# An mLSTM cell and a multiplicative feed-forward block: own outputs copied by ScalarE, y by DRAM from the eleventh unit, denominators in four passes

## The chip, the cores and the metric

The kernel runs on one core of a Trainium2 chip. The metric is the device time of one launch in microseconds (us); lower is better. All times below are us unless marked ns. The engines are named as the profile names them: PE is TensorE, DVE VectorE, ACT ScalarE, POOL GpSimd, SP SyncE, which issues most of the DMAs.

## What is computed

The reference has two parts. The first is a recurrence over 768 time steps for 4 batches of 8 heads of 40 columns:

```python
    for t in range(S):
        m_new = np.maximum(f_gate[:, :, t] + m, i_gate[:, :, t])
        f_stab = np.exp(f_gate[:, :, t] + m - m_new)
        i_stab = np.exp(i_gate[:, :, t] - m_new)
        C = f_stab * C + i_stab * outer(v[t], k[t])
        n = f_stab * n + i_stab * k[t]
        denom = max(abs(n . q[t]), 1.0)
        y[t] = sigmoid(o_gate[t]) * (C q[t]) / denom
```

The second takes x, which is y as 3072 tokens of 320 columns, and computes `((x @ w1) * (x @ w2)) @ w3 @ w_out`, with 1024 columns between. All is float32.

## The kernel before

**Units and stages.** The recurrence is cut into 24 units, one for each batch b and each 128 time steps c; unit n has c, b = divmod(n, 4). The main loop, `for s in range(len(n_up))`, has 32 turns; a turn is called a stage here. Stage s does the following for unit s: scores (q against k), weighting, state update. In the same stage it does for unit s - 1 the outputs, and for unit s - 2 or s - 3 the handing over of y to the feed-forward part. Beside this, a stage runs a share of the feed-forward part, by tables written out by hand: `n_up` (blocks of x @ w1 and x @ w2), `n_down` (blocks of the last product), `n_seven` and `n_out` (blocks done with seven products in place of eight), `n_cvt` (conversions of the weights w3 and w_out) and `n_fetch` (their loads). The order of the trace is the order on each engine's queue (`in_order` for PE, `keep_order` for the other engines), so an instruction that waits holds up all that stands behind it on its engine. This holds for SP's queue of DMAs too.

**Outputs of a unit** (`outputs`, `quarter_work`). PE leaves two things in the PSUM tile `cell[1]`: `pi`, what the state gives, and `ph`, what the unit's own 64-step halves give. DVE multiplies `pi` by the gate `gT` into `h` (L423), adds `ph` in four quarters of 64x164 (L430), and then makes the denominator. The last of 41 columns of each head is n . q, because the last column of `vbuf` is 1. L438 clears the sign bit, L440 takes max with 1 and doubles, L441 takes the reciprocal, L443 multiplies it by (o + 1), where o is a tanh, and L445 multiplies by `h` and writes `y`. Between these steps stand DVE's reading of the scores (L397), and the two state sums (L404, L414), the second of which waits for a product by POOL (L335).

**Handing over y.** There are two ways. For units under `NY` (15), `x_trans` turns y on PE, three 128x128 transposes into PSUM tile `px` (L95), and ACT copies it to `xT` (L486); POOL first doubles the last 64 columns (`twice`, L476). In stages 10 and later, stage s does this for unit s - 3, as the first PE work of the stage. For units from `NY` on, `send` writes y to DRAM (four DMAs on SP, L456 and L458), `get_back` reads it back in blocks (four DMAs, L465), and DVE turns 32x32 blocks (`x_turn`, L472). Stage s does this for unit s - 2: `send` is SP's first work of the stage, `get_back` stands behind the loads of k, v and o for unit s + 2, and `x_turn` stands on DVE behind `quarter_work`.

**Who reads xT.** One `xT` tile holds four units (a group). The 24 blocks of `ups` each read two units, a half of a group: blocks 16 to 19 read units 8 and 9, blocks 20 to 23 read units 10 and 11. By `n_up` stages 2 to 5 do one block and stages 6 to 15 two, so blocks 20 and 21 are done in stage 14. Groups 3 to 5 (units 12 to 23) are done by seven products: `token_sums` (L666, DVE) makes sums of a group's `xT` in stages 17, 21 and 25.

**SP's order in a stage** is written in the loop: `send(s - 2)`, `load_u(s + 3)` (tile pw, L159), k and v and o of unit s + 2 (L139, L153), `get_back(s - 2)`, `load_turned(s + 2)` (eight DMAs, tiles gates or q_all, L148), and last the fetches of w3 (tile raw, L184), eight DMAs a stage up to stage 12. A fetch needs a free `raw` buffer. One is freed by each conversion (`convert`: DVE L199, L200, then L248), and the conversions of a stage stand on DVE behind `turn` (L317, two transposes that make kT and qT of unit s + 1).

## Time and profile before

| | before |
|---|---|
| runs | 425.51, 426.51 and 427.06; median 426.51 |
| profiled execution | span 425.84; no time of its own beside the span is given |
| PE busy | 414.1 of 425.8 (97%), 5353 matmuls |
| DVE, ACT, POOL busy | 313.5 (74%), 150.1 (35%), 154.3 (36%) |
| mean granted TensorE clock | 0.996 |
| DMA | 51.15 MB, 120 GB/s in the mean |

The profile is of one execution. The span is from its first to its last instruction. A row of a timeline gives the start, the length, the engine, the line, what is written and read, and in brackets how long the engine was idle before it and what ended that; SPq is the DMA queue of SP, whose rows are the issuing and not the transfer. Rows of several instructions are merged (x4, x8), and their length reaches from the first's start to the last's end. A granted clock of 1.00 is TensorE's full speed.

Stages are found by their PE work. Stage 12 begins with the px transposes at 142.95, stage 13 at 158.94, stage 14 at 174.22, stage 15 at 189.51, stage 16 at 204.80, stage 17 at 220.07.

### The profile page before, as it was taken

The numbers are of one execution on the slowest core, as the hardware profiler recorded it, in microseconds if no ns is written. First come the engines' busy times: TensorE is split into PE (matmuls) and PEld (weight loads), VectorE is DVE, ScalarE is ACT, GpSimd is POOL, SyncE is SP. The second block draws the span as 40 slices with busy tenths as digits, with TensorE's granted clock in tenths as the row PEclk, the third lists the DMA queues.
The fourth block names the chain that finished last, engine by engine and source line by source line (L and its number), as shares of the span: only waits on it lengthen the run. The fifth ranks groups of instructions, "written<-read, shape, count | busy, mean of one in ns | idle before, by whom it ended". The sixth has DMA issues, their size and how long they took to land.

```text
span 425.8 us, 13079 instructions
## 1 busy us (share of the span) xinstructions
PE 414.1 (97%) x5353; PEld 335.3 (79%) x5353; DVE 313.5 (74%) x635; ACT 150.1 (35%) x404; POOL 154.3 (36%) x211
## 2 busy tenths in 40 slices
PE   7989989999999999999999999999999999999996
PEld 4768878888688788787777778788778879888896
DVE  6676986888949779778736966596868699575971
ACT  4766865567723623630433313032311110210000
POOL 4421342233303303303307751546453587542100
PEclk9989999999999999999999999999999999999999
DMA  8999998598977776985425675756421120000001
GB/s 186 204 173 245 214 144 140 134 193 180 215 183 154 166 182 135 181 164 105 89 80 130 153 141 121 142 133 117 87 44 36 35 39 2 31 2 31 2 32 62
DMA packets 135211, 51.15 MB, mean 120 GB/s; under 512 B 109360, under 2 KB 126960, under 8 KB 135152
## 3 DMA queue, kind: packets, MB, share of 16 engines
q1 hardware_dynamic: 131552, 46.29, 53.9%
q10 hardware_dynamic: 3600, 4.03, 2.7%
q8 instruction: 42, 0.69, 0.7%
q14 instruction: 17, 0.14, 0.1%
HBM read 44.50 MB, written 5.80 MB: 118 GB/s over the span
## 4 chain that ended last, share of the span: by engine, by line
PE 53%; issue 20%; DVE 7%; POOL 7%; SPq 7%; DMA 5%; ACT 1%; POOLq 0%; DVEq 0%
PE cell L92 17%; PE pa L92 12%; PE o L92 8%; PE pb L92 8%; PE p L92 3%; POOL pw L308 3%; SPq L184 3%; DVE w3T L666 2%; PE pt L95 1%; POOL vw L330 1%; SPq L148 1%; DMA raw<-in_moe_w_dram 1%; PE fill L92 1%; POOL raw L659 1%; POOL state L335 1%
## 5 line engine op out<-in xcount | busy, mean ns | idle before, releaser
L335 POOL TENSOR_TENSOR state<-state,decay 128x164 f32<-128x164 f32 x40 | 20.0, 500 | 154.8 <-DVE state L404 129.0
L92 PE MATMUL pa<-xT,w 128*128 128x256 f32 x240 | 60.4, 382 | 0.0
L92 PEld LDWEIGHTS pa<-xT,w 128*128 128x128 f32 x240 | 44.4, 190 | 6.8 <-DVE h L430 0.4
L303 ACT ACTIVATE pw<-pw,aT 128x64 f32<-128x64 f32 x184 | 46.4, 339 | 3.2 <-ACT o_sb L741 1.9
L92 PE MATMUL pb<-xT,w 128*128 128x256 f32 x192 | 45.4, 379 | 0.0
L729 POOL TENSOR_TENSOR ab<-ab,a_sb 128x512 f32<-128x512 f32 x22 | 29.4, 1356 | 32.2 <-DVE ab L684 32.2
L92 PEld LDWEIGHTS pb<-xT,w 128*128 128x128 f32 x192 | 36.4, 190 | 5.0
L711 POOL TENSOR_TENSOR wo<-wo 128x512 f32<-128x512 f32 x22 | 27.4, 1268 | 29.8 <-DVE wo L686 29.8
L92 PE MATMUL pa<-xT,wr 64*64 64x256 f32 x384 | 37.0, 386 | 0.5 <-DVE wr L200 0.5
L92 PE MATMUL wp<-wo,w3T 128*128 128x320 f32 x128 | 35.9, 433 | 1.1 <-DVE ab L639 0.6
L308 POOL TENSOR_SCALAR_AFFINE_SELECT pw<-pw 64x512 f32<-64x512 f32 x48 | 35.8, 746 | 3.0 <-ACT pw L303 1.2
L92 PE MATMUL pb<-xT,wr 64*64 64x256 f32 x384 | 36.4, 380 | 0.0
L92 PE MATMUL cell<-w3o,ab 128*128 128x320 f32 x128 | 35.4, 432 | 0.0
L638 ACT ACTIVATE a_sb<-pa 128x512 f32<-128x512 f32 x24 | 14.3, 598 | 59.0 <-PE pb L92 59.0
L639 DVE TENSOR_TENSOR ab<-pb,a_sb 128x512 f32<-128x512 f32 x24 | 16.4, 688 | 23.2 <-ACT a_sb L638 22.8
L92 PEld LDWEIGHTS wp<-wo,w3T 128*128 128x128 f32 x128 | 23.8, 190 | 10.5 <-DVE ab L639 0.8
L92 PEld LDWEIGHTS cell<-w3o,ab 128*128 128x128 f32 x128 | 24.3, 190 | 9.5
L92 PEld LDWEIGHTS pa<-xT,wr 64*64 64x64 f32 x384 | 18.9, 132 | 15.4 <-issue 8.8
L686 DVE SCALAR_TENSOR_TENSOR a_sb<-pa,wo 128x512 f32<-128x512 f32 x12 | 8.3, 689 | 29.8 <-PE pa L92 29.8
L430 DVE TENSOR_TENSOR h<-cell,h 64x164 f32<-64x164 f32 x88 | 28.6, 326 | 1.6
L92 PE MATMUL po<-w3o,ab 128*128 128x320 f32 x96 | 26.4, 433 | 0.0
L92 PEld LDWEIGHTS po<-w3o,ab 128*128 128x128 f32 x96 | 18.1, 190 | 7.3
(180 smaller groups left out, 846.4 us busy)
## 6 DMA issues: line engine op xcount, KB each, us to landing
raw<-in_moe_w_dram SPq DMA_DIRECT2D x64, 128.0 KB, 3.4
kbuf<-in_k_dram SPq DMA_DIRECT2D x24, 160.0 KB, 4.5
v_all<-in_v_dram SPq DMA_DIRECT2D x24, 160.0 KB, 4.9
o_in<-in_o_gate_dram SPq DMA_DIRECT2D x24, 160.0 KB, 4.8
pw<-U_d SPq DMA_DIRECT2D x28, 128.0 KB, 3.5
raw<-in_moe_w_dram SPq DMA_DIRECT2D x5, 512.0 KB, 6.7
raw<-in_moe_w_out_dram SPq DMA_DIRECT2D x8, 320.0 KB, 4.1
gates<-in_k_dram SPq DMA_DIRECT2D x28, 80.0 KB, 2.5
```

Of the source, the lines that this page charges most:

```text
L92: in_order(nc.tensor.matmul(out, lhsT=lhsT, rhs=rhs, start=start, stop=stop))
L184: nc.sync.dma_start(out=dst, in_=src)
L303: nc.scalar.activation(out=pw[:, h, :], in_=src[:, h, :], func=AF.Exp, bias=aT[:, c, b * H + h:b * H + h + 1])
L308: nc.gpsimd.affine_select(out=pw[r], in_=pw[r], compare_op=OP.is_ge, fill=0.0, base=0, pattern=[[0, H], [1, L]], channel_multiplier=-1)
L335: nc.gpsimd.tensor_tensor(out=new, in0=old, op=OP.mult, in1=decay[:, b * NP:(b + 1) * NP, 2 * c + x:2 * c + x + 1] .to_broadcast([P, NP, D1]))
L430: nc.vector.tensor_tensor(out=part, in0=ph[x][halves[e]], in1=part, op=OP.add)
L638: nc.scalar.mul(out=a_sb, in_=pa, mul=UP ** -2)
L639: nc.vector.tensor_tensor(out=ab_t[gr][j][:, fs[0]:fs[-1] + 1, t0:t0 + a_sb.shape[-1]], in0=pb, in1=a_sb, op=OP.mult)
L666: nc.vector.tensor_tensor(out=dst, in0=p, in1=q, op=OP.subtract)
L686: nc.vector.scalar_tensor_tensor(out=out, in0=p, scalar=UP ** -2, in1=q, op0=OP.mult, op1=OP.add)
L711: aside_by.tensor_tensor(out=kept[j][:, 1:4:2], in0=kept[j][:, 1:3], in1=kept[j][:, 3:4].to_broadcast([128, 2, TH]), op=OP.add)
L729: aside_by.tensor_tensor(out=t[:, f:FO:FH, :], in0=t[:, f:FO:FH, :], in1=a, op=OP.mult)
```

## The change

Three things change, and the diff is short enough to be shown whole.

1. `N_OWN = 10`: for units from 10 on, the gated `pi` goes to the tile `y` (as a scratch place), four ACT copies bring the quarters of `ph` from PSUM to `h`, and one DVE addition of 128x328 puts the two together. `y` is allocated at the start of `outputs` for all units.
2. `NY` goes from 15 to 10: units 10 to 14 too hand over y by DRAM.
3. For all units, the denominator is made in other steps. The last column of `vbuf` is 2 in place of 1, so the last column of `h` is 2 n . q. The steps are: reciprocal; the larger of the result and its negative; a pass over 128x320 that takes the minimum with 0.5 and multiplies into `h`; a pass over 128x320 that multiplies by (o + 1) into `y`.

```diff
-    N_DIAG = 2
+    N_DIAG, N_OWN = 2, 10
...
-    NY = 15
+    NY = 10
...
         h = sb.tile([P, H, D1], FP, name="h", tag="h")
-        nc.vector.tensor_tensor(out=h.rearrange("p (n two) d -> p two n d", two=2), in0=pi,
+        y = y_t[n] = sb.tile([P, DM + REM], FP, name="y", tag="y")
+        before = y[:, 0:H * D1].rearrange("p (h d) -> p h d", d=D1) if n >= N_OWN else h
+        nc.vector.tensor_tensor(out=before.rearrange("p (n two) d -> p two n d", two=2), in0=pi,
                                 in1=gT[:, c, hs].rearrange("p (n two) -> p two n", two=2).unsqueeze(3)
                                 .to_broadcast([P, 2, NP, D1]), op=OP.mult)
         if n < N_DIAG:
             nc.vector.tensor_tensor(out=h, in0=ph, in1=h, op=OP.add)
-        for x, e in quarters if n >= N_DIAG else ():
+        if n >= N_OWN:
+            for x, e in quarters:
+                nc.scalar.copy(out=h[halves[x], 0:H // 2] if x == e else h[halves[x], H // 2:H], in_=ph[x][halves[e]])
+            nc.vector.tensor_tensor(out=h, in0=before, in1=h, op=OP.add)
+        for x, e in quarters if N_DIAG <= n < N_OWN else ():
             part = h[halves[x], 0:H // 2] if x == e else h[halves[x], H // 2:H]
             nc.vector.tensor_tensor(out=part, in0=ph[x][halves[e]], in1=part, op=OP.add)
...
-            yield V.tensor_scalar(out=den.bitcast(U32), in0=h[:, :, D:D1].bitcast(U32), scalar1=0x7FFFFFFF, scalar2=None,
-                            op0=OP.bitwise_and)
-            yield V.tensor_scalar(out=den, in0=den, scalar1=1.0, scalar2=2.0, op0=OP.max, op1=OP.mult)
-            yield V.reciprocal(out=den, in_=den)
-            e = o_t.pop(n)
-            nc.vector.scalar_tensor_tensor(out=e, in0=e, scalar=1.0, in1=den.to_broadcast([P, H, D]), op0=OP.add, op1=OP.mult)
-            y_t[n] = sb.tile([P, DM + REM], FP, name="y", tag="y")
-            yield nc.vector.tensor_tensor(out=y_t[n][:, 0:DM].rearrange("p (h d) -> p h d", d=D), in0=h[:, :, 0:D],
-                                           in1=e, op=OP.mult)
+            yield V.reciprocal(out=den, in_=h[:, :, D:D1])
+            yield V.scalar_tensor_tensor(out=den, in0=den, scalar=-1.0, in1=den, op0=OP.mult, op1=OP.max)
+            v = h[:, :, 0:D]
+            yield V.scalar_tensor_tensor(out=v, in0=den.to_broadcast([P, H, D]), scalar=0.5, in1=v, op0=OP.min, op1=OP.mult)
+            yield V.scalar_tensor_tensor(out=y[:, 0:DM].rearrange("p (h d) -> p h d", d=D), in0=o_t.pop(n), scalar=1.0,
+                                         in1=v, op0=OP.add, op1=OP.mult)
...
-        nc.gpsimd.memset(vbuf[i][:, :, D:D1], 1.0)
+        nc.gpsimd.memset(vbuf[i][:, :, D:D1], 2.0)
```

The order of the changed kernel's instructions shows what this does to each engine. PE loses 15 transposes (five groups of px). ACT loses five copies of px and gains 14 groups of four copies of 64x164, each group ahead of the exponentials (L303) of the next unit. POOL loses five copies. SP gains 20 DMAs to DRAM and 20 back, in stages 12 to 16, at the places named above. DVE gains five block transposes.

## The prediction

> **What bounds the kernel now.** I read the page first, for shares and slices:

> ```profile
> PE 414.1 (97%) x5353; PEld 335.3 (79%) x5353; DVE 313.5 (74%) x635; ACT 150.1 (35%) x404; POOL 154.3 (36%) x211
> ...
> PE   7989989999999999999999999999999999999996
> ```

> PE is busy in nearly every slice. The view of waits, asked for PE alone, says how little it waits for others; these are the two entries that the change touches:

> ```profile
> PE px L95 <- DVE y L445: 1.2, 1, 1.2
> ...
> PE pa L92 <- DVE w3T L666: 0.4, 1, 0.4
> ```

> So from stage 2 on the span is PE's queue, and time is won by taking work from that queue or lost by making it wait. A faster DVE is worth nothing by itself. The question for each edit is therefore: what does PE wait for then, and when does that come? PE's timeline at the start of stage 14:

> ```profile
> 174.22 0.55 PE L95 MATMUL px<-ident,y 128*128 128x128 f32 x3
> 174.61 4.47 PE L92 MATMUL wp<-wo,w3T 128*128 128x320 f32 x16
> 178.92 1.46 PE L92 MATMUL pa<-xT,w 128*128 128x256 f32 x6
> ```

> The px here turns unit 11. The pa that starts at 178.92 is block 20 of `ups`, the first reader of unit 11's xT. This is the place that decides, as follows.

> **Part 1, work taken from PE (gain).** A px group holds the queue from 174.22 to 174.61, 0.39. Units 10 to 14 lose theirs: 5 x 0.39 = 1.95. Of these, units 10 and 11 stand ahead of block 20, units 12 to 14 behind it.

> **Part 2, own outputs by ACT, and four passes (DVE and ACT).** DVE's timeline for unit 10 before:

> ```profile
> 142.60 0.49 DVE L423 TENSOR_TENSOR h<-cell,gT 128x328 f32<-128x328 f32 x1
> 143.12 1.34 DVE L430 TENSOR_TENSOR h<-cell,h 64x164 f32<-64x164 f32 x4
> ...
> 146.15 0.33 DVE L414 TENSOR_TENSOR state<-cell,state 128x164 f32<-128x164 f32 x1 [0.47 <-POOL state L335]
> 146.40 0.76 DVE L443 SCALAR_TENSOR_TENSOR o_in<-o_in,den 128x320 f32<-128x320 f32 x1
> 147.20 0.82 DVE L445 TENSOR_TENSOR y<-h,o_in 128x320 f32<-128x320 f32 x1
> ```

> The four additions (1.34) go. In the changed kernel's order with its waits, ACT's first copy waits for DVE's multiply of the same unit (the old L423), though it reads only `ph`; so the copies do not lie beside the multiply but after it. No row has this copy. Bounds: the exponentials of 128x64 follow each other every 0.25 (2.01 for eight), the po copies of 128x320 take 0.43; four copies cost 1.0 to 1.7. I take 4 x 0.29 = 1.2, interpolated by columns between the exponentials' 0.25 and the kT and qT copies of 128x512, which start 0.48 apart. The addition of 128x328 is like L423, 0.5. So h is ready 1.7 after the multiply in place of 1.34: 0.35 later. The short passes lose one (0.17). The long pass now stands ahead of L414 and covers its 0.47 wait for POOL. Net per unit from 10 on: +0.35 - 0.17 - 0.47 = -0.3; below 10: -0.6. PE waits for neither, except at 242, where `token_sums` made it wait 0.4 (0.58 with the start-up of the matmul). DVE comes 0.3 earlier there, and xT of unit 15 is no longer behind; I take -0.5.

> ACT's exponentials of stage 11 began at 141.85 and would begin at 143.1 + 1.2 = 144.3, 2.4 later. Behind them stands the copy of px for unit 9, which ended at 146.82 and would end at 149.2, while PE wants it at 148.34: 0.8 of waiting, in stage 12. It lies ahead of block 20 and is swallowed by the larger wait there. The first-stage wait of 1.2 for y shrinks by some 0.6, but conversions held by loads (ACT waits for raw at 42.48 and 44.48) stand before stage 3's end; I take 0.1.

> [...] Here L443 (two float32 sources) at 24.60 took 0.49 and L445, a tensor_tensor, took 0.49 at 25.13. [...]

> **Part 3, y by DRAM for units 10 and 11 (loss).** SP's timeline, stages 11 to 13, then stage 17, which already works in the new way:

> ```profile
> 151.06 3.89 SPq L184 DMA_DIRECT2D raw<-in_moe_w_dram  x8
> 155.06 1.09 SPq L159 DMA_DIRECT2D pw<-U_d  x2
> ...
> 167.00 3.89 SPq L184 DMA_DIRECT2D raw<-in_moe_w_dram  x8
> 171.01 1.09 SPq L159 DMA_DIRECT2D pw<-U_d  x2
> ...
> 224.90 1.28 SPq L456 DMA_DIRECT2D y_d<-y  x2
> 226.22 1.15 SPq L458 DMA_DIRECT2D y_d<-y  x2
> ...
> 231.05 3.05 SPq L465 DMA_DIRECT2D yb<-y_d  x4
> ```

> ```profile
> 235.87 0.58 DVE L472 STREAM_TRANSPOSE xT<-yb 128x384 f32<-128x384 f32 x1
> ```

> Unit 15's way from the first `send` to the block transpose took 224.90 to 235.87, 10.97; unit 16's 238.72 to 249.54, 10.8. Between stand four sends (2.5), the loads of pw, k, v and o, and the reads back, which land behind o. The new units have the same DMAs between, so 10.9 is the price of the way. SP does not reach it early, because the stage before ends with the raw fetches, which wait for DVE's conversions (first group of four DMAs after the first L200, second after the second).

> Step by step. Stage 11's fetches end 0.3 earlier, at 154.65. Unit 10: send at 154.65, block transpose at 154.65 + 10.9 = 165.55, done 166.1. DVE is free for it at 163.99 - 0.3 + 0.7 (the late px of unit 9) = 164.4 and waits. Behind the transpose stand `turn` and the two conversions of stage 12. Before, the second L200 ended at 169.11, 5.12 after y; now at 166.1 + 5.12 = 171.2. The last four fetches follow it, 1.8, to 173.0. Unit 11: send at 173.05, block transpose at 183.95, done 184.5. So block 20 starts at 184.55, not 178.92: +5.6, in which the px of units 10 and 11 and ACT's 0.8 are already contained. PE, ready at 178.92 - 0.78 + 0.7 = 178.85, idles 5.7. Bounds: if unit 10's transpose holds up no conversion, the send of unit 11 is at 170.65 and block 20 at 182.1, +3.2; if each way takes 13.5 (each 2.6 more, as where SP's issues are held up: unit 18's reads back took 5.21 to issue), +10.8.

> Units 12 to 14 have time: their first reader is `token_sums` of stage 17. DVE's delay of stage 13 (kT and qT of unit 14 by 186.6, wanted by PE after 193) is inside PE's own delay.

> **Clock.** PE's idle time costs more than itself. The view by windows for the start of this kernel:

> ```profile
> 19.98:23.40 3.42, 2.23 (x52) 1.74 (x52) 2.81 (x9) 2.39 (x8) 2.14 (x4) 1.00 1.21 164
> 23.40:26.83 3.43, 3.43 (x30) 1.93 (x31) 3.05 (x9) 2.79 (x6) 0.53 (x2) 0.50 0.96 146
> ```

> A stretch of 3.42 with PE busy for 2.23 was followed by one of 3.43 at a granted clock of 0.50. An idle time of 5.7 should give at least one such stretch. If all of it falls on work it costs 3.43 / 2 = 1.7; it can fall half on the idle time (0.9) or be followed by a second (3.4 at most). I take 1.7, and 0 to 2.7 for the range. [...]

> **Sum**, against the span 425.84: +5.6 (block 20) - 3 x 0.39 (px of units 12 to 14) - 0.5 (at 242) + 1.7 (clock) - 0.1 = +5.5, span 431.3. The median of the runs, 426.51, lies 0.67 above the span; with it 432.0. Low end: 3.2 - 1.17 - 0.5 + 0 = +1.5, 428.0. High end: 10.8 - 1.17 - 0.5 + 2.7 = +11.8, 438.3.

> **Rivals.**
> 1. *The way by DRAM is hidden, PE only loses work.* Unit 11's transpose would have to be done by 178.1. For it: y of unit 11 exists at 164, and DRAM's own part is short (sends land in 2.2, reads in 2.0). Against: SP comes to the send only behind the fetches. Price: -1.95 - 0.5 - 0.1 = -2.55, 424.0, faster. It decides if SP sends unit 11 before 178.1 - 11.5 = 166.6, which is ahead of stage 12's fetches.
> 2. *ACT is what is late, not DRAM.* Only the late px of unit 9 costs, 0.8, or up to 2.0 with copies at 0.43 each: -2.55 + 0.8 to 2.0 = 424.8 to 426.0, no change or a little faster. For it: ACT's copies wait for DVE. Against: this touches one stage only, since no px is left behind it.
> 3. *The delay grows.* Both ways take 13.5 and the clock stays at half for two stretches: 437 to 438. For it: in stages 13 and 14 DMA share was 0.70 and 0.95. Against: it needs both units slow.

> **Chances.** Forecast (428.0 to 436, centre 432.0): 0.76. Rival 1: 0.09. Rival 2: 0.08. Rival 3: 0.07. By the bound of 0.5% (424.4 to 428.6, about what a measurement of this kernel can tell from no change): faster 0.10 (rival 1 and a little of 2), same 0.09 (the rest of rival 2, the low end of the forecast), slower 0.81. For 8 in 10 the range runs from 427.0 to 437.0: the forecast, and rival 3 in part.

> **What would show it.** Right: PE idle of 4 to 8 just ahead of pa in stage 14, released by DVE's L475 (the block transpose); SP's second new send at 172 to 174; a granted clock of 0.50 in the 3.4 behind it; pa and px of unit 9 meeting in a wait under 1. Wrong: no gap there, or a gap that DVE's h or ACT's copies end; or a block transpose that ran before 178.

## The result, and the profile after

Before 426.75 (median of 4 runs, 425.51 to 427.06), after 436.53 (median of 4 runs, 436.11 to 438.70): the change makes the kernel slower, ratio 1.025, 95% interval 1.021 to 1.029. The forecast was 432.0, range 427 to 437. The side and the place were right; the loss is 9.8 in place of 5.5. The profiled execution after has a span of 436.95, with 438.70 the longest of the four; its clock is 0.992.

The page after, against the two rows shown of before:

```profile
PE 414.3 (95%) x5338; PEld 334.3 (77%) x5338; DVE 292.4 (67%) x574; ACT 164.0 (38%) x455; POOL 155.8 (36%) x206
...
PE   7898799999999899589999999999999999999997
...
PEclk9999999999999999979999999999999999999999
```

VectorE lost 21 of its busy time (313.5 to 292.4) and ScalarE gained 14 (150.1 to 164.0), as the change says. TensorE's sum is unchanged (414.1 and 414.3), since slower matmuls at block 20 (2.0 more) hide the five px groups that left (0.38 each). PE's digits 5 and 8 and the clock's 7 are one place: the seventeenth and eighteenth slice, 175 to 197. The view of waits for PE names it:

```profile
PE pa L92 <- DVE xT L475: 6.8, 1, 6.8
PE pa L92 <- DVE wr L200: 2.3, 1, 2.3
PE cell L92 <- ACT qT L325: 1.9, 1, 1.9
...
PE pa L92 <- ACT xT L489: 1.4, 1, 1.4
...
PE cell L92 <- DVE qT L317: 1.0, 1, 1.0
```

The first entry is block 20 waiting for unit 11's block transpose (new L475), which did not exist before. The second and third lie at 41 and 49, where the loads of the start end late in this execution; they are no part of what follows. The fourth is ScalarE's late copy of px for unit 9, the fifth lies in stage 18, at 251. TensorE's timeline around the first:

```profile
175.72 4.57 PE L92 MATMUL wp<-wo,w3T 128*128 128x320 f32 x16
187.11 3.75 PE L92 MATMUL pa<-xT,w 128*128 128x256 f32 x8 [6.81 <-DVE xT L475]
```

Block 20 started at 178.92 before. Its first eight matmuls take 3.75; eight of the same kind take 1.89 where the clock is full (before at 178.92, after at 192.54).

Set against the same instructions of before, the profiled execution after divides so: +0.6 at 143; +7.6 from there to the start of block 20; +2.0 in its first matmuls; -0.8 for px of units 12 to 14; +1.8 in stages 17 to 20; nothing behind. That is +11.1, as the spans have it (436.95 against 425.84).

### The profile page after: what moved, and what is told of

It is laid out like the page before. It is cut to its first block, busy times and chain, and to the rows that moved or that the text cites. A ratio compares the mean times of both kernels' runs of the same rounds, so it can differ in the third digit from the quotient of the medians.

```text
span 436.9 us, 13106 instructions
## 1 busy us (share of the span) xinstructions
PE 414.3 (95%) x5338; PEld 334.3 (77%) x5338; DVE 292.4 (67%) x574; ACT 164.0 (38%) x455; POOL 155.8 (36%) x206
## 4 chain that ended last, share of the span: by engine, by line
PE 51%; SPq 17%; issue 9%; DVE 8%; DMA 8%; POOL 5%; ACT 1%; DVEq 0%; POOLq 0%; ACTq 0%
PE cell L92 14%; PE pa L92 12%; PE o L92 8%; PE pb L92 7%; SPq L184 6%; SPq L139 5%; PE p L92 4%; SPq L153 3%; DMA raw<-in_moe_w_dram 2%; POOL raw L662 2%; PE wp L92 2%; PE po L92 2%; DMA wo<-in_moe_w_dram 2%; SPq L159 1%; SPq L468 1%
## 5 line engine op out<-in xcount | busy, mean ns | idle before, releaser
L335 POOL TENSOR_TENSOR state<-state,decay 128x164 f32<-128x164 f32 x40 | 22.7, 566 | 162.3 <-DVE state L404 144.2
L92 PE MATMUL pa<-xT,w 128*128 128x256 f32 x240 | 62.5, 392 | 8.2 <-DVE xT L475 6.8
L92 PEld LDWEIGHTS pa<-xT,w 128*128 128x128 f32 x240 | 45.3, 195 | 16.2 <-issue 7.6
L303 ACT ACTIVATE pw<-pw,aT 128x64 f32<-128x64 f32 x184 | 46.4, 337 | 0.3
L92 PE MATMUL pb<-xT,w 128*128 128x256 f32 x192 | 45.8, 381 | 0.2 <-DVE w L200 0.2
L92 PEld LDWEIGHTS pb<-xT,w 128*128 128x128 f32 x192 | 36.7, 192 | 5.6 <-DVE w L200 0.6
L92 PE MATMUL pa<-xT,wr 64*64 64x256 f32 x384 | 37.0, 386 | 2.3 <-DVE wr L200 2.3
L92 PE MATMUL wp<-wo,w3T 128*128 128x320 f32 x128 | 36.3, 437 | 0.4 <-DVE ab L642 0.4
L92 PE MATMUL pb<-xT,wr 64*64 64x256 f32 x384 | 36.4, 380 | 0.0
L308 POOL TENSOR_SCALAR_AFFINE_SELECT pw<-pw 64x512 f32<-64x512 f32 x48 | 34.6, 721 | 4.9 <-ACT pw L303 3.4
L92 PE MATMUL cell<-w3o,ab 128*128 128x320 f32 x128 | 35.4, 432 | 0.0
L92 PEld LDWEIGHTS pa<-xT,wr 64*64 64x64 f32 x384 | 18.9, 132 | 17.2 <-issue 8.8
L92 PEld LDWEIGHTS cell<-w3o,ab 128*128 128x128 f32 x128 | 24.3, 190 | 9.5
L92 PEld LDWEIGHTS wp<-wo,w3T 128*128 128x128 f32 x128 | 23.8, 190 | 10.0 <-DVE ab L642 0.6
L432 ACT COPY h<-cell 64x164 f32<-64x164 f32 x56 | 16.2, 290 | 34.1 <-DVE y L425 33.6
L92 PE MATMUL po<-w3o,ab 128*128 128x320 f32 x96 | 26.5, 435 | 0.0
L475 DVE STREAM_TRANSPOSE xT<-yb 128x384 f32<-128x384 f32 x14 | 8.0, 575 | 26.7 <-DMA yb<-y_d 26.7
L92 PEld LDWEIGHTS po<-w3o,ab 128*128 128x128 f32 x96 | 18.1, 190 | 7.4
```

The lines of the kernel that those rows point to most:

```text
L92: in_order(nc.tensor.matmul(out, lhsT=lhsT, rhs=rhs, start=start, stop=stop))
L303: nc.scalar.activation(out=pw[:, h, :], in_=src[:, h, :], func=AF.Exp, bias=aT[:, c, b * H + h:b * H + h + 1])
L308: nc.gpsimd.affine_select(out=pw[r], in_=pw[r], compare_op=OP.is_ge, fill=0.0, base=0, pattern=[[0, H], [1, L]], channel_multiplier=-1)
L335: nc.gpsimd.tensor_tensor(out=new, in0=old, op=OP.mult, in1=decay[:, b * NP:(b + 1) * NP, 2 * c + x:2 * c + x + 1] .to_broadcast([P, NP, D1]))
L432: nc.scalar.copy(out=h[halves[x], 0:H // 2] if x == e else h[halves[x], H // 2:H], in_=ph[x][halves[e]])
```

## The experiments

Each run was timed in five rounds beside the kernel before on the same chip. The table gives the ratio to before with its 95% interval and, from the profile, what TensorE's queue lost against before in three stretches, read at the same instructions: from a pa at 100 (of before) to the second pa of stage 14, from there to the own outputs (`cell` from `v_all` and `pw`) of stage 17, and from there to TensorE's last matmul. Stretches are used because the first 100 differ by -3.7 to +0.7 from the one profile of before, whatever else was changed.

| kernel | ratio (interval) | 100 to stage 14 | to stage 17 | to the end |
|---|---|---|---|---|
| after | 1.025 (1.021 to 1.029) | +9.5 | -0.8 | +1.8 |
| e1 four passes alone | 0.997 (0.995 to 0.999) | -0.2 | 0.0 | 0.0 |
| e2 after without own copies | 1.020 (1.016 to 1.024) | +8.8 | -0.8 | +1.2 |
| e3 after without DRAM | 1.008 (1.005 to 1.011) | +3.1 | 0.0 | +1.1 |
| e4 every send early | 1.030 (1.027 to 1.033) | +1.8 | -0.8 | +13.2 |
| e5 sends of units 10 to 13 early | 1.024 (1.021 to 1.027) | +1.7 | -0.9 | +9.2 |
| e6 the same, no own copies | 1.020 (1.018 to 1.023) | -0.2 | -0.8 | +10.6 |
| e7 after, 14 fillers | 1.034 (1.030 to 1.039) | +12.7 | -0.9 | +2.6 |
| e8 DRAM from unit 12, no own copies | 1.015 (1.011 to 1.019) | 0.0 | -0.8 | +7.1 |
| e9 e8, out by GpSimd | 0.997 (0.994 to 1.000) | -0.3 | -0.8 | +0.2 |
| e10 e6, out by GpSimd | 1.009 (1.005 to 1.012) | +0.5 | -0.8 | +3.4 |
| e11 after, 7 fillers | 1.025 (1.020 to 1.030) | +7.8 | +0.8 | +3.4 |
| e12 after, out by GpSimd | 1.024 (1.020 to 1.028) | +9.0 | -0.8 | +1.4 |
| e14 e1, out by GpSimd | 0.998 (0.995 to 1.002) | +0.1 | 0.0 | +0.1 |
| e15 e9, but DRAM from unit 10 | 1.017 (1.014 to 1.021) | +8.0 | -0.9 | +0.1 |
| e16 e9, but DRAM from unit 11 | 1.009 (1.006 to 1.013) | +5.2 | -0.9 | +0.2 |

**The three parts apart: e1, e2, e3.** All edits are against the kernel after:

```diff
-    N_DIAG, N_OWN = 2, 10
+    N_DIAG, N_OWN = 2, 24      # e1 and e2: no own copies
-    NY = 10
+    NY = 15                    # e1 and e3: units 10 to 14 stay on TensorE
```

> The kernel before with one part of the change: denominators in four passes (ones of v become 2.0). Own outputs stay quarter additions on VectorE, y of units 10 to 14 stays on TensorE. Theory (the loss is the way by DRAM and what hangs on it): VectorE gets some 0.2 to 0.3 shorter per unit, TensorE hardly waits for it, so 0 to -0.6 against before. Rival (the four passes are themselves slow or late, the loss is VectorE's): +1 or more.

> The changed kernel without ScalarE's own copies (quarter additions on VectorE for all units), y of units 10 to 14 by DRAM. Theory: the gap ahead of block 20 in stage 14 stays at 6 to 7.5, released by the block transpose, the half clock behind it stays, the gap of 1 in stage 18 stays; only the 1.06 of stage 12 goes, and it was swallowed by the larger wait anyway. So 435 to 437, the same as the changed kernel within 1. Rival (ScalarE's copies make units late and so the way by DRAM): the gap falls by 2 or more, 433 or less.

> The changed kernel without the way by DRAM for units 10 to 14: ScalarE's own copies and the four passes stay, TensorE turns y of units 10 to 14 as before. Theory: no gap in stage 14 over 1.5, no half clock there; ScalarE's exponentials and the copy of px behind them are late by about 2.4, which costs TensorE about 1 once in stage 12 and again where block 20 reads unit 11 (0 to 1); against before +0.3 to +2, 427 to 428.5. Rival (ScalarE's copies are the main loss): +4 or more, 430.5 and above.

e1: 424.61 against 426.06. The four passes cost nothing; from 100 on TensorE's queue gains 0.2, so that the gain of 0.3%, if it is one, lies in the first stages. All profiles with the four passes but that of the kernel after reach 100 earlier than before does, by 0.7 to 3.7, which would fit; after's comes 0.7 later, and with one profile of before no run here settles it. e2: 434.91, gap 6.5 ahead of block 20, also after unit 11's transpose. The rival (ScalarE makes the way late) falls. e3: 429.45, more than the theory's 428.5, less than the rival's 430.5. The mechanism is the one that was named, in stages 12 and 14; a third loss, in stages 19 and 20, has another (below, at stages 17 to 20). ScalarE's timeline of e3 in stage 13 and TensorE's at block 20:

```profile
172.90 1.19 ACT L432 COPY h<-cell 64x164 f32<-64x164 f32 x4 [1.16 <-DVE y L425]
174.12 2.02 ACT L303 ACTIVATE pw<-pw,aT 128x64 f32<-128x64 f32 x8
...
178.62 0.46 ACT L489 COPY xT<-px 128x384 f32<-128x384 f32 x1
```

```profile
172.68 0.55 PE L95 MATMUL px<-ident,y 128*128 128x128 f32 x3
173.06 4.47 PE L92 MATMUL wp<-wo,w3T 128*128 128x320 f32 x16
179.14 1.99 PE L92 MATMUL pa<-xT,w 128*128 128x256 f32 x8 [1.61 <-ACT xT L489]
```

The four copies wait 1.16 for VectorE's multiply, the exponentials follow them, and the copy of px for unit 11 comes at 178.62, when TensorE has been ready since 177.5. TensorE loses 1.1 in stage 12, 1.9 at block 20 with the start-up of pa, and 1.1 in stages 19 and 20.

**The order on SP: e4, e5, e6.** The send of a unit and its reading back move to the end of the stage that makes y, ahead of the raw fetches:

```diff
+        if NY <= s - 1 < NU:       # e4; e5 and e6: NY <= s - 1 <= 13
+            send(s - 1)
+            get_back(s - 1)
         while todo and fetched < (n_fetch[s] if s < len(n_fetch) else converted + 4):
```

and are dropped at the head of the next stage for those units. e6 has N_OWN = 24 as well.

> The changed kernel with one move: the send of a unit and its reading back are issued at the end of the stage in which its y is made, ahead of that stage's raw fetches, instead of at the start of the next stage. Same instructions. Theory (SP's order decides, the way itself is short): send of unit 11 near 165 instead of 174.6, its block transpose no longer late; the gap ahead of block 20 falls from 6.8 to under 1.5, the half clock behind it goes, and the gap in stage 18 (send of unit 15 behind SP's held loads) goes too: 424 to 427.5. Rival (the way by DRAM is long by itself, about 11 to 12 wherever it starts, or the reading back stays behind held loads): gap of 3 or more, 431 or above.

> The early send of the fourth run for units 10 to 13 alone; from unit 14 on send and reading back stand where the changed kernel has them. Own copies and four passes stay. Theory (SP's order around the raw fetches makes the gap of stage 14, and in the fourth run it was the loads of the next stages, queued behind the waiting send, that were late): the gap ahead of block 20 is about 1, released by the block transpose or by ScalarE's copy, no half clock, and no gap of 5.9 in stage 17; what stays is two waits of 1.0 to 1.2 for late units and the 1 to 1.8 of stages 17 to 19, less 1.4 for five px groups: 428 to 430. Rival (early sends only move the loss to a later stage): 433 or more.

> The same as the run with early sends for units 10 to 13, without ScalarE's own copies (quarter additions on VectorE for all units). Theory (own copies are a loss of their own, because they make ScalarE's later work late): no wait in stage 12, none over 0.5 ahead of block 20; about 1.2 stays in stage 17 or 18; the den-only kernel (424.6) less 1.4 for px, plus 1.2: 423 to 425. Rival (own copies cost nothing once DRAM is in time): within 1 of the run with own copies.

In all three the gap ahead of block 20 is gone (0.9, 0.9 and 0.5 after the transpose) and so is the half clock there. So it was the place of the send on SP's queue that made it. But 439.39, 435.47 and 433.69 are no faster than without the move: the forecasts for the total fell, and the rival "early sends only move the loss" has the totals. In stage 17 or 18 TensorE now waits 5.2 to 5.7 for VectorE's qT, and the clock halves behind that. e6 against e5 is faster by 0.4%, the price of own copies once more.

**Where the loss went: e8, e9, e14.** e8 takes away the readers in stage 14 instead: with NY = 12 the first unit by DRAM is read in stage 17.

> Four passes, no own copies by ScalarE, y by DRAM from unit 12 on (units 10 and 11 turned by TensorE as before). Units 12 to 14 are first read in stage 17. Theory (only the readers in stages 12 to 14 make the way by DRAM dear): no gap over 0.5 in stage 14, three px groups less (-0.8 to -1.1), and the gap of stage 18 of 1.1 stays, because unit 14's send is on SP's queue in stage 16: 424 to 425, the same as the den-only kernel within 0.6. Rival (any unit by DRAM delays SP's loads and costs in the stages where it is sent): 427 or more.

The theory was wrong by 7, and the rival has the time: 431.71. Nothing is lost up to stage 17, then, in stage 18, TensorE waits 4.6 for qT. The chain of work that ended last, cut to this stretch, follows it back:

```profile
233.11 0.44 ACT o_sb L744
233.54 0.02 issue
233.56 3.73 DMA out_dram<-o_sb
237.29 0.02 issue
237.30 0.02 SPq L468
...
238.66 2.35 DMA q_all<-in_k_dram
241.01 1.04 DVE kT L317
242.05 0.92 DVE qT L317
```

SP issues a reading back at 237.30, 0.01 after a write of finished rows to `out`, which ScalarE had issued, has landed. SP's queue has nothing to do with these rows. The records of the issues in the traces say why. In before and after the issues of SP and ScalarE (411 and 451) use the same eight semaphores in turn, in one order over both queues. On the seven semaphores whose landings are all on record, every issue but the first of each (352 and 388) starts behind the landing of the transfer that used its semaphore last, eight places ahead. Where that is a write to `out`, SP starts 0.01 to 0.02 behind it: at 259.60 after 259.59 in before, at 228.14 after 228.12 in after. Here the write that ScalarE issued at 233.56 and the reading back that SP issued at 237.35 use the same one. A write to `out` is issued when TensorE has finished its block, late in the stage, so whatever SP issue stands eight places behind it waits for TensorE and then for the landing, 2.4 to 4.2 here. Which issue that is depends on how many there are, and y by DRAM adds eight to each unit's stage. In e4, e5 and e6 too one load of q_all stands for such a write, 6.2, 6.9 and 3.4. e9 takes this tie away:

```diff
-            nc.scalar.dma_start(out=out[t0:t0 + P, :], in_=o_sb)
+            nc.gpsimd.dma_start(out=out[t0:t0 + P, :], in_=o_sb)
```

> The kernel with y by DRAM from unit 12 on (four passes, no own copies), with one change: the writes of finished rows to out are issued by GpSimd instead of ScalarE. The trace of the run before it shows SP's issues standing until such a write has landed (214.75, 237.29, 242.02), because in the built program the issues of SP and ScalarE take turns at eight semaphores, and an issue waits for the transfer eight places ahead of it, whichever queue that is on; GpSimd's transfers have others. Theory (this tie is what holds SP in stages 16 and 17): the gap of 4.6 in stage 17 and the half clock behind it go, 423.5 to 425.0, that is the den-only kernel less 0 to 1.1. Rival (transfers or SP's issues are simply too many in these stages): a gap of 3 or more stays, 429 or more.

> Control: the den-only kernel (y of units 10 to 14 on TensorE) with the writes to out issued by GpSimd. Theory: in that kernel no stall of TensorE hangs on the tie, so no change, 424 to 425. If it is faster by 1 or more, the runs with GpSimd's writes owe that much to it and not to the way by DRAM; if slower, GpSimd's own work is late by the issues.

e9: 425.75 against 425.51, ratio down from 1.015 to 0.997 by this line; the theory's 423.5 to 425.0 is missed by 0.7, but the ratio is that of e1, and its gap of 4.6 and the half clock are gone. SP's timeline at the send of unit 14, in e8 and then in e9:

```profile
207.01 1.24 SPq L459 DMA_DIRECT2D y_d<-y  x2
208.30 6.86 SPq L461 DMA_DIRECT2D y_d<-y  x2
215.32 1.13 SPq L159 DMA_DIRECT2D pw<-U_d  x2
```

```profile
207.34 1.24 SPq L459 DMA_DIRECT2D y_d<-y  x2
208.63 1.15 SPq L461 DMA_DIRECT2D y_d<-y  x2
209.95 1.13 SPq L159 DMA_DIRECT2D pw<-U_d  x2
```

Two small sends take 6.86 there and 1.15 here; in e8 a write to `out` lands at 214.75. That GpSimd's transfers have other semaphores, as e9's expectation says, is seen by this effect alone. The control e14 (425.57, no change) shows that GpSimd's writes win nothing where TensorE turns y itself. So the tie is the cause of e8's loss.

**Early sends without the tie: e10.**

> Early sends for units 10 to 13, four passes, no own copies, and the writes to out issued by GpSimd. Theory: no gap in stage 14 (early sends) and none over 0.7 in stages 16 to 19 (no shared semaphores): the den-only kernel less five px groups of 0.28 net, 422.5 to 424.0, the fastest so far. Rival (early sends delay SP's loads by themselves): 4 or more in stage 16, 428 or more.

Ratio 1.009, where e6 has 1.020: most of the loss from stage 17 on goes, but 3.4 stay, and the expectation fell. The rival has the time (430.57) but not its gap of 4: the waits for qT are 1.3 and 0.7, and the clock halves behind the first. In its SP timeline the reading back of unit 13 waits 2.5 for the send to land (issues end at 202.18, the send's last parts land at 204.6 and 204.7, the reading back is issued at 204.71), the loads stand behind it, and the send of unit 14 comes at 215.60, where e9 has it at 207.34. Early sends thus do hold loads by themselves, by less than e6 made it look.

**How many units by DRAM: e15, e16, and e12.** e9 with NY = 10 and with NY = 11; e12 is the kernel after with GpSimd's writes.

> y by DRAM from unit 10 on, four passes, no own copies, writes to out by GpSimd: the third of a series that differs only in the first unit that goes by DRAM (12: 425.75, 15: 425.57). Theory: 6 to 7 ahead of block 20 and 1.7 to 2 of half clock, less 1.4 for px, no gap in stages 16 to 19: 7 to 8 over the one from unit 12, 432 to 434. Rival (the way by DRAM also costs in later stages without the tie): 435 or more.

> The same series from unit 11 on: unit 10 is turned by TensorE again, unit 11 goes by DRAM. Theory (unit 10's block transpose, waiting 1.6 for its reading back, holds the conversions of stage 12, these hold the raw fetches, and these the send of unit 11): without unit 10's way the gap ahead of block 20 shrinks by 1.5 to 2.5, from 6.5 to 4 to 5, half clock 1 to 2 behind it: 429 to 432. Rival (unit 11's own way alone makes the gap): the gap stays within 0.7 of the one from unit 10, 432 to 434.

> The changed kernel with one change: the writes to out are issued by GpSimd, so that SP's issues no longer take turns with them at the eight semaphores. Theory: the gap ahead of block 20 (6.8) and the half clock stay, since no write to out is issued before stage 16; the 1.03 in stage 18, where SP stood 4.2 for such a write, goes; what own copies cost in stages 17 to 19 (about 1) stays. 0.7 to 1.8 faster than the changed kernel: 434.5 to 436, with before at 426.5. Rival (the tie costs nothing while TensorE is 9 late anyway): no change.

From unit 12, 11 and 10 on: 425.75, 429.97, 433.05. e16's gap ahead of block 20 is 3.6, e15's 6.3. VectorE's timeline, first e15, then e16:

```profile
164.74 0.58 DVE L475 STREAM_TRANSPOSE xT<-yb 128x384 f32<-128x384 f32 x1 [1.95 <-DMA yb<-y_d]
...
169.70 0.69 DVE L200 CUSTOM_DVE_ANT_0 w<-raw,w 128x1024 uint16<-128x1024 uint16 x1
...
183.53 0.58 DVE L475 STREAM_TRANSPOSE xT<-yb 128x384 f32<-128x384 f32 x1 [5.73 <-DMA yb<-y_d]
```

```profile
165.59 0.69 DVE L200 CUSTOM_DVE_ANT_0 w<-raw,w 128x1024 uint16<-128x1024 uint16 x1
...
179.43 0.58 DVE L475 STREAM_TRANSPOSE xT<-yb 128x384 f32<-128x384 f32 x1 [3.02 <-DMA yb<-y_d]
```

Unit 10's transpose, waiting for DRAM, holds the conversions of stage 12; the second L200 comes at 169.70 instead of 165.59 (1.6 of this is e15's later start), the raw fetches and unit 11's send follow it. So the delay of unit 10 is handed on to unit 11: the theory of the series holds, and the gap shrinks by 2.7, a little more than its 1.5 to 2.5. e12: 436.00 against 425.43, ratio 1.024, 0.1% from after's: no change that the times could tell, as the rival said. In its profile the 1.0 at qT in stage 18 is gone, but `token_sums`, which that wait had covered, now makes TensorE wait 0.8.

**The clock: e7, e11.** Filler matmuls that nobody reads, ahead of block 20:

```diff
+        if s == 14:
+            warm(14)               # e11: warm(7)
         now = [ups.pop(0) for _ in range(n_up[s])]
```

> The changed kernel with 14 filler matmuls of 128x512 on TensorE ahead of block 20, in the idle time of 6.8; their result is used by nobody. Theory (the idle time makes the clock gate halve the clock for two stretches, 1.98): block 20 starts when it started before, the granted clock behind it is 1.0, the first eight pa take 1.9 and not 3.7; 1.5 to 2.2 under the changed kernel, 434.0 to 435.0. Rival (the slow matmuls behind the gap are the price of loads in flight, not of idle time): no change, 436 to 437.

> The changed kernel with 7 filler matmuls of 128x512 (0.86 each, 6.0) ahead of block 20, so that they end before unit 11's transpose. Theory (TensorE's idle time halves the clock behind it): block 20 starts where it did in the changed kernel, granted clock 1.0 behind it, 1.5 to 2.2 faster than the changed kernel: 434 to 435. Rival (the half clock is not from idle time): 436 to 437 with the first eight pa still at 3.7.

e7's edit was mis-sized: a filler shows as two matmuls of 0.43, so 14 of them take 12.0, and block 20 starts later than after, at 189.47; what it shows is that the granted clock stays 1.0 and that nothing is lost in block 20's matmuls. e11 has the right size. The view by windows around block 20, after and then e11 (PE busy and PEld busy lead, then VectorE, ScalarE, GpSimd; the granted clock stands third from the end):

```profile
180.73:184.15 3.42, 0.00 (x0) 0.00 (x0) 0.00 (x0) 1.36 (x3) 1.47 (x3) 1.00 1.22 171
184.15:187.56 3.41, 0.45 (x1) 0.48 (x2) 1.18 (x2) 0.00 (x0) 0.00 (x0) 0.50 0.71 153
187.56:190.98 3.42, 3.42 (x9) 2.70 (x9) 3.35 (x6) 0.00 (x0) 0.00 (x0) 0.50 0.67 127
```

```profile
180.00:183.40 3.40, 2.94 (x7) 0.95 (x5) 0.19 (x1) 0.00 (x0) 0.00 (x0) 1.00 0.91 155
183.40:186.80 3.40, 2.96 (x14) 2.62 (x15) 3.33 (x6) 0.00 (x0) 0.00 (x0) 1.00 0.68 161
186.80:190.20 3.40, 3.40 (x17) 3.00 (x16) 3.15 (x4) 0.00 (x0) 0.00 (x0) 1.00 0.45 101
```

In e11 block 20 starts after the same transpose, 7.7 late (7.6 in the kernel after), and its first eight pa take 1.99 at full clock. By this mark, the theory's, the 2.0 come from the idle time. Yet the time, 436.94, is the rival's, and the ratio is after's own, 1.025: in the profiled execution a stall of 1.5 with no releaser ("issue") stands at 194.6, and 1.6 more than after is lost from stage 17 on. Why the saving does not reach the end stays open.

## Why the prediction was right and wrong, point by point

**What bounds the kernel: right.** VectorE's busy time fell by 21, and by 8 in e1 (313.5 to 305.2), which gains some 0.3% if anything. The time is lost where TensorE's queue waits.

**Part 1, px: right in kind, 0.1 too high.** Each group that leaves takes 0.38, and where two long groups then follow each other, the start of pa gives back 0.10.

**Part 2, own copies and passes: right on the durations, wrong on the reach.** Unit 10 after:

```profile
143.21 0.49 DVE L425 TENSOR_TENSOR y<-cell,gT 128x328 f32<-128x328 f32 x1
144.96 0.50 DVE L433 TENSOR_TENSOR h<-y,h 128x328 f32<-128x328 f32 x1 [1.26 <-ACT h L432]
...
146.50 0.48 DVE L447 SCALAR_TENSOR_TENSOR h<-den,h 128x320 f32<-128x320 f32 x1
147.34 0.33 DVE L414 TENSOR_TENSOR state<-cell,state 128x164 f32<-128x164 f32 x1 [0.36 <-POOL state L335]
147.58 0.77 DVE L448 SCALAR_TENSOR_TENSOR y<-o_in,h 128x320 f32<-128x320 f32 x1
```

The four copies took 1.19 (1.2 was taken), the addition 0.50; from L425 to the end of y it is 5.14 in place of 5.42, -0.28 for the forecast's -0.3, and 4.74 in e1, -0.7 for -0.6. One detail was wrong: the long pass does not cover L414's wait for GpSimd, which shrinks from 0.47 to 0.36 only. The second long pass, now a `scalar_tensor_tensor` with two float32 sources, is no slower for it, as the prediction's rows at 24.60 and 25.13 (0.49 each) had it: the two long passes take 0.48 and 0.77, where they took 0.76 and 0.82. The price in stage 12 was 1.1 instead of 0.8. Rival 2 said that this touches one stage only. With px gone that holds for units 10 and 11, but in stages 19 and 20 own copies take another 1.0 (e3: +1.1 where e1 has 0.0): there matmuls into `cell` wait for VectorE's addition into the state (L414), which comes later; this had no term.

**Part 3, the way by DRAM: right in mechanism, mis-sized by 2.0.** The step was the price of one way, 10.9, taken from units 15 and 16. SP's timeline after shows both new ways:

```profile
151.33 3.90 SPq L184 DMA_DIRECT2D raw<-in_moe_w_dram  x8
155.27 1.28 SPq L459 DMA_DIRECT2D y_d<-y  x2
...
160.29 3.12 SPq L153 DMA_DIRECT2D o_in<-in_o_gate_dram  x1
163.50 2.07 SPq L468 DMA_DIRECT2D yb<-y_d  x4
...
170.68 3.91 SPq L184 DMA_DIRECT2D raw<-in_moe_w_dram  x8
174.64 1.24 SPq L459 DMA_DIRECT2D y_d<-y  x2
...
181.76 2.35 SPq L468 DMA_DIRECT2D yb<-y_d  x4
```

Unit 10's send starts at 155.27 (154.65 was forecast; the 0.6 by which this execution is late anyway) and its transpose at 167.14: 11.87. Here one issue, o_in, took 3.12, against 1.02 in stage 17 of before. Unit 11: 174.64 to 186.38, 11.74. In e15 and e16 three such ways took 11.0, 11.3 and 11.3: a way that starts behind eight raw fetches took 0.1 to 1.0 more than the 10.9 of units 15 and 16, which have none ahead of them, and two ways in a row pay it twice. That the fetches are the cause is argued, not shown: that the DMA engines were busier there (a share of 1.22 from 180.73 to 184.15, against 0.31 in stage 17 of before) would fit as well. So block 20 stood at 187.11 in place of 184.55. The other end of the range, "no conversion held up", gave +3.2; e16, which is that case with px of unit 10 back on TensorE, measured +3.4.

**Clock: 2.0 for 1.7, in part by luck.** The term was one stretch of 3.43 that falls on work as a whole. There were two of 3.41, of which the first lies on 3.0 of idle time: 3.9 / 2 = 1.9. The 0 at the low end of its range is shown by no run: the idle times of 3.6 to 6.8 were followed by half clock for 3.41 or 6.83. In the kernel after a window with PE busy for 0.00 (180.73 to 184.15) stands ahead of the half clock, which ends with a window busy for 3.42 of 3.42. But e16's window ahead of its half clock had PE busy for 0.47 of 3.41, and this one of e10 for 2.11, nearly all of it in the matmuls of 40 to 64 rows and columns:

```profile
226.21:229.62 3.41, 2.11 (x129) 1.91 (x128) 3.36 (x6) 2.70 (x10) 3.27 (x5) 1.00 0.68 160
229.62:233.03 3.41, 3.41 (x19) 2.19 (x8) 2.99 (x10) 0.00 (x0) 1.43 (x3) 0.50 0.62 161
```

So in these two no wholly idle window stood ahead. Nor does busy time alone tell what followed, so a row like the prediction's, 2.23 of 3.42, could not settle the term. In the profiles the clock changes in steps of 3.41 (before: 17.07 at full, 3.41 at half, 399.36 at full, which are 5, 1 and 117 of them; after: 52, 2 and 72); counted in these, e3 has a window with 1.80 (176.07 to 179.48), all in matmuls of 128x128, the kernel after one with 2.39 (249.00 to 252.42) and e2 one with 2.34 (246.73 to 250.14), both nearly all in the small matmuls that e10's has, and the clock stays 1.0 behind all three, while it halves behind one of e4 with 2.49 (18.84 to 22.25). That the size of the matmuls weighs in is a guess from these few windows and wasn't tried by itself.

**Stages 17 to 20: the term with the wrong sign.** The forecast took -0.5 for `token_sums`; measured is +1.8, the largest miss of the sum. TensorE's timeline after:

```profile
251.34 0.69 PE L92 MATMUL cell<-qT,kT 40*64 40x64 f32 x32 [1.03 <-DVE qT L317]
...
257.24 1.99 PE L92 MATMUL cell<-w3T,raw 128*128 128x256 f32 x8 [0.22 <-DVE state L414]
```

The wait for `token_sums` is gone only because TensorE waits 1.0 for qT just ahead of it: e12, which does not, has 0.8 there, where before has 0.4. Two causes had no term. One is own copies, as above. The other is the tie: after, SP's load of v stands from 223.94 to 228.14, behind a write to `out` that lands at 228.12. Without own copies 1.2 stay (e2), without the tie 1.4 (e12), without both 0.1 (e15): the two hide behind each other in part. The 0.4 of the tie are too little for the times to tell. The prediction had such a wait before its eyes, without the cause. SP's timeline before:

```profile
254.94 1.13 SPq L159 DMA_DIRECT2D pw<-U_d  x2
259.60 0.38 SPq L139 DMA_DIRECT2D kbuf<-in_k_dram  x1
```

Nothing is issued for 3.5, until a write to `out` lands at 259.59; and of the 5.21 of unit 18's reads back, from which the prediction took its upper bound, 2.5 are a wait for another, which lands at 279.09. With the gap of stage 14 closed the tie costs 7 (e8), so the prediction's rival 1, "hidden, 424.0", could not have been had by SP's order alone (e4 to e6).

**Rival 3, "the delay grows", came in part.** It asked for two ways of 13.5 and half clock for two stretches. Both ways were slower, by 1.0 and 0.8 in place of 2.6 each, and the half clock lasted two stretches.

**Sum** in the terms of the forecast: block 20 +7.6 for +5.6; clock +2.0 for +1.7; px behind it -0.8 for -1.2; stages 17 to 20 +1.8 for -0.5; the start +0.6 for -0.1, which no run ties to the change. Together +11.1 for +5.5 in the profiled execution. The steps that failed are thus two: the price of a way, 10.9 where 11.9 and 11.7 were paid one behind the other, and the term for stages 17 to 20, which left out what own copies do to L414 and what a write to `out` does to SP.

## What to carry to other kernels

In this kernel a way through DRAM costs what stands ahead of it on its queue more than what its transfers take (11.87 and 11.74 for the first two after, with 2.2 from a send's issue to its landing and 2.5 for a read): ask where in the queue the send stands, what it waits for, and whether its late end holds what the next send waits for. Once the first reader is late enough, further delays hide behind it, so closing one gap may only uncover the next; find it by moving the readers (e8) rather than the sends. DMA issues of different engines were tied by shared semaphores here (two sends took 6.86 in e8 and 1.15 in e9): look for an issue that starts when a foreign transfer lands, and try another engine's queue (e9).
